# Moving the background decodings of the last two matrices to other units of a three-pass expert kernel

## The chip, the cores and the metric

The kernel runs on one core of a Trainium2 chip. The metric is the time of one execution on the device in microseconds; a version's time is the median over several runs.

## What is computed

Three blocks follow each other: block-causal attention, a mixture of experts whose gate is balanced over the tokens, and a two-matrix block with a SoLU and a layer norm. Only what the change touches is quoted.

```python
def _moe_ref(x, w_gate, w1, w2):          # x 2304 x 512, 8 experts of 512 x 1024 x 512
    ...                                    # P: gate, balanced in 8 rounds
    for e in range(E):
        h = np.maximum(x @ w1[e], 0.0)
        ye = h @ w2[e]
        out += P[:, e:e + 1] * ye

def _moe2_ref(x, w_in, w_out, g_ln):      # w_in 512 x 1024, w_out 1024 x 512
    h = x @ w_in
    ...                                    # SoLU, then layer norm with g_ln
    return (ln @ w_out).astype(np.float32)
```

## The kernel before

**Number format.** TensorE multiplies operands that are split into two parts (a cast and a remainder), three matmuls for each product. `split_weights` makes the two parts: ScalarE casts (L445), GpSimd subtracts (L446).

**The experts.** The tokens go through the experts in three passes of 768 tokens. An expert is halved into two units, so that a pass has the units u = 2 to 15 behind the two that are done with the attention. In every unit the first layer is computed with seven block products in place of eight (`first_layer`, L712): TensorE makes the products (L708 to L710), VectorE combines them (L720, tiles u2, u3, vu2, vu3; the trace cuts the digits), ScalarE copies r1 (L733), and `hidden` makes the hidden tiles. In the first pass these are h tiles (L750 on ScalarE, L751 on VectorE), and the second layer is an ordinary one (`second_layer`, L853: six outputs of twelve matmuls, accumulated by VectorE in L868). In the second and third passes a hidden tile is weighted by the gate into `hb` (L762 on VectorE), combined and split into seven `hf` tiles (L769 on ScalarE, L770 and L773 on GpSimd, one L773 on VectorE), and the second layer has seven products as well (`second_products`, L804): 14 groups of six matmuls, each into a PSUM tile `yps`, which VectorE adds to the accumulator (L816) or, in a pass's first unit, ScalarE copies there (L814).

**Order.** The second products of a unit stand behind the first layer of the next, so that a unit's stretch on TensorE holds 84 matmuls of a first layer and the 84 of the second layer of the unit before. A list of 28 units, `work`, runs through the second and third passes. In between, `finish_pass` combines the accumulators of a pass (L831), multiplies the sums y0 of the first, ordinary units with the gate (L848 on GpSimd) and adds them (L850 on VectorE), and `spread_x` (L599 and others) makes the seven combined token tiles of the next pass. Each engine executes its instructions in the order in which they stand in its queue.

**The decodings.** w_in and w_out of the last block come as 64-bit words. `late` lists 32 half matrices of 128x256 words, 16 of w_in and 16 of w_out. `decode` (L455) makes one of them into the two-part format and stores it to DRAM, from where the last block loads it: a load of 256 KB by SyncE into a tile of the ring `wr` (11 tiles, shared with the weight tiles W, of which a unit takes 14); on VectorE the seven instructions L465, L474, L468, L471, L477, L479, L483 on 128x256, for w_out an eighth, L485; the cast L445 on ScalarE; the subtraction L446 on GpSimd; a store of 256 KB (L488). The scratch tiles a64, b64 and f64 are there once each. Nothing needs a decoded matrix before the last block, from about 1745 us on.

**Who calls it.** The first pass calls it between the layers of a unit (n = u - 2 = 0 to 13), the two later passes behind the first layer of the unit with the number n = 14 to 41:

```python
    def late_decode(n):
        if 8 <= n < 40:
            decode(*late[n - 8])
    ...
        late_decode(u - 2)          # first pass
    ...
            late_decode(n + 14)     # second and third pass
```

So before the change there is one decoding for each n from 8 to 39: n = 8 to 13 in the last six units of the first pass, n = 14 to 27 in the second pass, n = 28 to 39 in all but the last two units of the third.

Of the kernel before, what the change touches and what calls it, by code (L numbers as in the profile page):

```python
# [24 lines left out]
def build(ctx, tc, qT, kT, v, w_gate, w1, w1s, w2, w_in, w_out, g_ln, out):  # L25
# [36 lines left out]
    def r32(ap):  # L62
        return ap.bitcast(F32)
# [380 lines left out]
    def split_weights(t, raw):  # L444
        nc.scalar.copy(t[:, 0, :], raw)  # L445
        nc.gpsimd.tensor_tensor(t[:, 1, :], raw, r32(t[:, 0, :]), op=ALU.subtract)  # L446
# [8 lines left out]
    def decode(i, half, src, scale=None):  # L455


        pair = wr.tile([P, 2, 512], F32R, tag="wr", name="w64")
        raw = pair[:, 0, :].bitcast(U32)
        nc.sync.dma_start(raw, src)  # L460
        raw = raw.rearrange("p (n w) -> p n w", w=2)
        lo, hi = raw[:, :, 0], raw[:, :, 1]
        a = dec.tile([P, 256], U32, tag="a64", name="a64")
        b = dec.tile([P, 256], U32, tag="b64", name="b64")
        nc.vector.tensor_scalar(  # L465
            a, hi, 3, 0x3FFFFFFF, op0=ALU.logical_shift_left, op1=ALU.bitwise_and
        )
        nc.vector.scalar_tensor_tensor(  # L468
            a, hi, 0xC0000000, a, op0=ALU.bitwise_and, op1=ALU.bitwise_or
        )  # L470
        nc.vector.scalar_tensor_tensor(  # L471
            a, lo, 29, a, op0=ALU.logical_shift_right, op1=ALU.bitwise_or
        )
        nc.vector.tensor_scalar(  # L474
            b, lo, 28, 1, op0=ALU.logical_shift_right, op1=ALU.bitwise_and
        )
        nc.vector.tensor_tensor(a, a, b, op=ALU.add)  # L477

        nc.vector.tensor_scalar(  # L479
            b, hi, 1, 28, op0=ALU.logical_shift_left, op1=ALU.logical_shift_right  # L480
        )
        f = dec.tile([P, 256], F32, tag="f64", name="f64")
        nc.vector.scalar_tensor_tensor(f, b, 7.0, r32(a), op0=ALU.is_ge, op1=ALU.mult)  # L483
        if scale is not None:
            nc.vector.tensor_scalar_mul(f, f, scale)  # L485
        t = pair[:, 1, :].rearrange("p (s n) -> p s n", s=2)
        split_weights(t, f)
        nc.sync.dma_start(wdram[i, :, :, half * 256 : half * 256 + 256], r32(t))  # L488
# [473 lines left out]
    late = []  # L962
    for i in range(16):
        for half in range(2):

            if i < 8:
                a = i % 2 * 1024 + half * 512
                late.append((i, half, w_in[i // 2 * P : i // 2 * P + P, a : a + 512]))
            else:
                c = i - 8  # L970
                late.append((i, half, w_out[c * P : c * P + P, half * 512 : half * 512 + 512], gsc[:, c : c + 1]))
    def late_decode(n):
        if 8 <= n < 40:
            decode(*late[n - 8])


    ws = second_weights(2)
    for u in range(2, 16):
        hs = {}
        first_layer(W, X, plain_hidden(hs))  # L980
        if u < 15:
            W, nws = first_factors(u + 1, stg), second_weights(u + 1)
        else:
            X = {}
            run(spread_x(1, X))
            W = load_factors(2, 0)
        late_decode(u - 2)
        second_layer(u, 0, ws, hs)
        ws = nws
# [9 lines left out]
    for n, (p, u) in enumerate([*work, (3, 2)]):  # L999
        if n < len(work):  # L1000
            if u % 2 == 0:
                Pb = gate_weights(u // 2, p)
            R = {}
            hidden, steps = weighted_hidden(R, Pb)
            first_layer(W, X, hidden)
            late_decode(n + 14)

        if before:
            for _ in second_products(*before):
                next(steps, None)  # L1010
        run(steps)
        if n < len(work):
            if n + 1 < len(work):
                if work[n + 1][0] > p:
                    X = {}
                    run(spread_x(p + 1, X))
                W = load_factors(work[n + 1][1], 0)
            before = load_factors(u, 1), R, u == 2
        if u == 2 and p > 1:
            finish_pass(p - 1)  # L1020
# [161 lines left out]
```

## Time and profile before

| | |
|---|---|
| median of three runs | 1983.21 us (1980.9 to 1985.86) |
| the profiled execution | 1983.74 us, its span 1982.0 us |
| TensorE busy | 1898.4 us, 96% of the span |
| VectorE, GpSimd, ScalarE busy | 1454.0, 1163.6, 743.3 us |
| mean granted TensorE clock | 0.985 |

The profile shows one execution. Busy time counts an engine's own instructions; the granted clock is the share of TensorE's full 2.4 GHz that it was given, so that 0.5 is its lower level of 1.2 GHz. The three passes of the units 2 to 15 stand between 472 and 1745 us; the first pass ends at about 905 us, the second at about 1335 us. The trace cuts a digit at the end of a name (hb for hb and y0's slots, w for w64, a and b for a64 and b64).

### The profile page before, as it was taken

How to read it: one execution, taken by the hardware profiler on the slowest of the kernel's cores; microseconds unless marked ns; L12 is line 12 of the kernel's file. 1: busy time of each engine (PE TensorE's matmuls, PEld its weight loads, DVE VectorE, ACT ScalarE, POOL GpSimd, SP SyncE). 2: the span in 40 equal slices, each digit the busy share in tenths (PEclk: the TensorE clock that was granted, in tenths of full speed). 3: DMA queues.
4: the chain of work that ended last, by engine and by line, in shares of the span. 5: the costliest groups of instructions: out<-in, count | busy, mean ns of one | idle time of the engine just before them, and what ended most of it. 6: DMA issues, size and time to landing. Idle time of an engine off the chain costs nothing.

```text
span 1982.0 us, 31143 instructions
## 1 busy us (share of the span) xinstructions
PE 1898.4 (96%) x10487; PEld 1762.7 (89%) x10487; DVE 1454.0 (73%) x3104; ACT 743.3 (38%) x1555; POOL 1163.6 (59%) x920
## 2 busy tenths in 40 slices
PE   5899999889999999999999999998999999989999
PEld 4688998788998989889999999987999999978887
DVE  5868677666777769888867667797866766678774
ACT  5766657433434434343222222222222122224332
POOL 7775645455766667656666676668757557631000
PEclk8999999999999999999999999998999999989999
DMA  8765554337888888879787787876788787851100
GB/s 233 189 181 150 153 148 117 134 99 270 298 303 309 292 315 311 297 251 370 271 289 265 272 279 257 288 259 238 282 285 294 257 278 274 307 205 44 47 28 32
DMA packets 197758, 454.61 MB, mean 229 GB/s; under 512 B 20432, under 2 KB 78432, under 8 KB 197472
## 3 DMA queue, kind: packets, MB, share of 16 engines
q1 hardware_dynamic: 197600, 452.63, 67.3%
q8 instruction: 84, 1.38, 0.3%
q14 instruction: 74, 0.61, 0.1%
HBM read 295.72 MB, written 128.52 MB: 214 GB/s over the span
## 4 chain that ended last, share of the span: by engine, by line
PE 77%; DVE 9%; DMA 4%; POOL 4%; issue 3%; ACT 1%; SPq 1%; DVEq 0%; POOLq 0%; ACTq 0%
PE yps L708 5%; PE yps L710 5%; PE yps L709 5%; PE psb L709 4%; PE psb L708 4%; PE psb L710 4%; PE yps L862 3%; PE yps L864 3%; PE yps L863 3%; PE psc L710 2%; PE psc L708 2%; PE psc L709 2%; PE psa L708 2%; PE psa L710 2%; PE psa L709 2%
## 5 line engine op out<-in xcount | busy, mean ns | idle before, releaser
L770 POOL TENSOR_TENSOR hf<-hb,hf 128x768 fp32r<-128x768 f32 x196 | 368.4, 1895 | 94.9 <-ACT hf L769 94.9
L769 ACT CAST hf<-hb 128x768 fp32r<-128x768 f32 x196 | 160.5, 836 | 490.4 <-POOL hb L773 158.5
L708 PE MATMUL yps<-hf,W 128*128 128x384 f32 x784 | 268.1, 342 | 10.5 <-DVE hb L762 8.2
L709 PE MATMUL yps<-hf,W 128*128 128x384 f32 x784 | 267.1, 341 | 0.0
L710 PE MATMUL yps<-hf,W 128*128 128x384 f32 x784 | 263.8, 341 | 0.0
L773 POOL TENSOR_TENSOR hb<-hb 128x768 f32<-128x768 f32 x84 | 158.8, 1891 | 161.6 <-DVE hb L762 160.1
L816 DVE TENSOR_TENSOR acc<-yps,acc 128x384 f32<-128x384 f32 x364 | 192.6, 549 | 67.6 <-PE yps L710 66.9
L446 POOL TENSOR_TENSOR w<-raw,w 128x512 fp32r<-128x512 f32 x96 | 125.8, 1323 | 109.3 <-ACT w L445 104.6
L708 PE MATMUL psb<-X,W 128*128 128x384 f32 x504 | 169.7, 337 | 1.4 <-ACT acc L814 1.4
L709 PE MATMUL psb<-X,W 128*128 128x384 f32 x504 | 169.3, 336 | 0.0
L710 PE MATMUL psb<-X,W 128*128 128x384 f32 x504 | 167.7, 335 | 0.0
L708 PEld LDWEIGHTS yps<-hf,W 128*128 128x128 f32 x784 | 149.0, 190 | 13.1 <-DVE hb L762 9.8
L709 PEld LDWEIGHTS yps<-hf,W 128*128 128x128 f32 x784 | 149.1, 190 | 0.0
L720 DVE TENSOR_TENSOR u<-psb,r 128x384 f32<-128x384 f32 x168 | 91.1, 550 | 79.1 <-PE psb L710 71.4
L710 PEld LDWEIGHTS yps<-hf,W 128*128 128x128 f32 x784 | 148.7, 190 | 0.0
L862 PE MATMUL yps<-w,h 128*128 128x512 f32 x336 | 133.3, 397 | 5.5 <-DVE acc L868 2.7
L233 POOL TENSOR_SCALAR e<-e,sv 128x128 f32<-128x128 f32 (+2 forms) x144 | 81.1, 567 | 95.6 <-DVE sv L229 31.4
L446 POOL TENSOR_TENSOR W<-raw,W 128x512 fp32r<-128x512 f32 x84 | 117.7, 1416 | 29.7 <-ACT W L445 29.7
L864 PE MATMUL yps<-w,h 128*128 128x512 f32 x336 | 132.6, 395 | 0.0
L863 PE MATMUL yps<-w,h 128*128 128x512 f32 x336 | 132.5, 394 | 0.0
L1102 POOL TENSOR_SCALAR lh<-ln 128x1024 f16<-128x1024 f32 x18 | 19.1, 1059 | 187.4 <-DVE ln L1099 65.2
L708 PE MATMUL psa<-X,W 128*128 128x384 f32 x336 | 113.5, 338 | 2.9 <-ACT W L445 1.5
(233 smaller groups left out, 5330.5 us busy)
## 6 DMA issues: line engine op xcount, KB each, us to landing
W<-fd SPq DMA_DIRECT2D x392, 512.0 KB, 5.6
fd<-W SPq DMA_DIRECT2D x154, 512.0 KB, 5.2
fd<-w SPq DMA_DIRECT2D x84, 256.0 KB, 4.7
raw<-in_w1s SPq DMA_DIRECT2D x56, 256.0 KB, 5.5
raw<-in_w SPq DMA_DIRECT2D x14, 1024.0 KB, 6.9
raw<-in_w SPq DMA_DIRECT2D x40, 256.0 KB, 3.4
kh<-khigh SPq DMA_DIRECT2D x64, 144.0 KB, 2.9
kl<-kraw SPq DMA_DIRECT2D x64, 144.0 KB, 2.7
```

The lines of the kernel that those rows point to most:

```text
L446: nc.gpsimd.tensor_tensor(t[:, 1, :], raw, r32(t[:, 0, :]), op=ALU.subtract)
L708: nc.tensor.matmul(ps, wh, xl, start=start and kc == 0, stop=False, skip_group_check=True)
L709: nc.tensor.matmul(ps, wh, xh, start=False, stop=False, skip_group_check=True)
L710: nc.tensor.matmul(ps, wl, xh, start=False, stop=stop and kc == 1, skip_group_check=True)
L720: nc.vector.tensor_tensor(to, bank[g, a], tmp[g, "r1" if a == "b" else name[1:]], op=ALU.add)
L769: nc.scalar.copy(hi, a)
L770: nc.gpsimd.tensor_tensor(lo, a, r32(hi), op=ALU.subtract)
L773: eng.tensor_tensor(o, a, b, op=ALU.subtract)
L816: nc.vector.tensor_tensor(a, ps, a, op=ALU.add)
L862: nc.tensor.matmul(ps, hl, ws[c][:, 0, :], start=c == 0, stop=False)
L863: nc.tensor.matmul(ps, hh, ws[c][:, 1, :], start=False, stop=False)
L864: nc.tensor.matmul(ps, hh, ws[c][:, 0, :], start=False, stop=c == 3)
```

## The change

Which n has a decoding is now written out in a list. None of the first pass's units (n = 0 to 13) has one, nor have the last unit of the second pass (n = 27) and the first two of the third (n = 28, 29). The last two units (n = 40, 41) have one each, and the seven units n = 16, 18, 20, 22, 24, 33 and 36 two each, whose second stands directly behind the first in the code. The order of the 32 half matrices stays the same. All else of the kernel is unchanged.

```diff
--- before.py
+++ after.py
@@ -969,9 +969,13 @@
                 c = i - 8
                 late.append((i, half, w_out[c * P : c * P + P, half * 512 : half * 512 + 512], gsc[:, c : c + 1]))
+
+    when = sorted([*range(14, 27), *range(30, 42), 16, 18, 20, 22, 24, 33, 36])
+
     def late_decode(n):
-        if 8 <= n < 40:
-            decode(*late[n - 8])
+        for i, w in enumerate(when):
+            if w == n:
+                decode(*late[i])
```

The first place is VectorE's queue in the second unit of the third pass (n = 29), where TensorE makes that unit's first layer and then the second products of n = 28. Before, these rows stood around the last hidden tiles hb of that first layer (psc is one of its PSUM tiles, y0 the sum of the first, ordinary units that finish_pass adds):

```order
L720 TENSOR_TENSOR psc_14656<-psc_14656,u2_14614 128x384
L465 TENSOR_SCALAR a64_14713<-w64_14711 128x256
L474 TENSOR_SCALAR b64_14714<-w64_14711 128x256
L773 TENSOR_TENSOR hb_14368<-hb_14368,hb_14332 128x768
L762 SCALAR_TENSOR_TENSOR hb_14701<-psc_14656,pb_14254 128x384
L468 SCALAR_TENSOR_TENSOR a64_14713<-w64_14711,a64_14713 128x256
L720 TENSOR_TENSOR psc_14667<-psc_14667,u2_14623 128x384
L850 TENSOR_TENSOR acc_101<-acc_101,y0_14579 128x768
L471 SCALAR_TENSOR_TENSOR a64_14713<-w64_14711,a64_14713 128x256
L762 SCALAR_TENSOR_TENSOR hb_14701<-psc_14667,pb_14254 128x384
L477 ISA a64_14713<-a64_14713,b64_14714 128x512
L479 TENSOR_SCALAR b64_14714<-w64_14711 128x256
```

Now the same stretch reads:

```order
L773 TENSOR_TENSOR hb_14336<-hb_14336,hb_14300 128x768
L762 SCALAR_TENSOR_TENSOR hb_14636<-psb_14568,pb_14222 128x384
L720 TENSOR_TENSOR psc_14608<-psc_14608,u2_14566 128x384
L720 TENSOR_TENSOR psc_14619<-psc_14619,u2_14575 128x384
L762 SCALAR_TENSOR_TENSOR hb_14653<-psc_14608,pb_14222 128x384
L762 SCALAR_TENSOR_TENSOR hb_14653<-psc_14619,pb_14222 128x384
L850 TENSOR_TENSOR acc_101<-acc_101,y0_14536 128x768
L720 TENSOR_TENSOR u2_14856<-psb_14849,r1_14838 128x384
```

The decoding's rows are gone. Three of the four L850 now stand further ahead, among the u and vu rows of that unit; the fourth stands behind the last hb.

The second place is VectorE's queue among the second products of a doubled unit. Before, in a unit with one decoding (it stands ahead of these rows), the adds followed each other:

```order
L816 TENSOR_TENSOR acc_101<-yps_10991,acc_101 128x384
L816 TENSOR_TENSOR acc_101<-yps_11002,acc_101 128x384
L762 SCALAR_TENSOR_TENSOR hb_10958<-psc_10924,pb_10541 128x384
L816 TENSOR_TENSOR acc_101<-yps_11010,acc_101 128x384
L816 TENSOR_TENSOR acc2_10038<-yps_11021,acc2_10038 128x384
L816 TENSOR_TENSOR acc2_10038<-yps_11029,acc2_10038 128x384
```

Now, in the unit n = 18, the second decoding's rows stand between the adds:

```order
L816 TENSOR_TENSOR acc_101<-yps_11236,acc_101 128x384
L465 TENSOR_SCALAR a64_11215<-w64_11213 128x256
L474 TENSOR_SCALAR b64_11216<-w64_11213 128x256
L816 TENSOR_TENSOR acc_101<-yps_11247,acc_101 128x384
L762 SCALAR_TENSOR_TENSOR hb_11188<-psc_11154,pb_11074 128x384
L816 TENSOR_TENSOR acc_101<-yps_11255,acc_101 128x384
L468 SCALAR_TENSOR_TENSOR a64_11215<-w64_11213,a64_11215 128x256
L816 TENSOR_TENSOR acc2_9948<-yps_11266,acc2_9948 128x384
L471 SCALAR_TENSOR_TENSOR a64_11215<-w64_11213,a64_11215 128x256
L816 TENSOR_TENSOR acc2_9948<-yps_11274,acc2_9948 128x384
L477 ISA a64_11215<-a64_11215,b64_11216 128x512
L816 TENSOR_TENSOR acc2_9948<-yps_11287,acc2_9948 128x384
```

From the second add on there is a decoding row after nearly every add, until the seven are through; the first decoding stands where the single one stood. The seven doubled units read alike, but for L485 behind the seven in n = 33 and 36 (w_out), and n = 16, whose first decoding stands a row or two further behind.

The third place is ScalarE's queue at the beginning of the second pass, around the cast L445 of the decoding n = 15; L814 are the copies of that pass's first accumulators. Before:

```order
L814 COPY acc2_10038<-yps_10454 128x384
L814 COPY acc2_10038<-yps_10462 128x384
L445 CAST w64_10360<-f64_10370 128x256
L814 COPY acc_101<-yps_10474 128x384
L814 COPY acc_101<-yps_10482 128x384
L814 COPY acc_101<-yps_10493 128x384
L814 COPY acc_101<-yps_10501 128x384
L733 COPY r1_10550<-psa_10543 128x384
```

Now:

```order
L814 COPY acc2_9948<-yps_10344 128x384
L445 CAST w64_10270<-f64_10280 128x256
L814 COPY acc2_9948<-yps_10352 128x384
L769 CAST hf_10361<-hb_10243 128x768
L814 COPY acc2_9948<-yps_10364 128x384
L814 COPY acc2_9948<-yps_10372 128x384
L814 COPY acc_101<-yps_10384 128x384
L814 COPY acc_101<-yps_10392 128x384
L814 COPY acc_101<-yps_10403 128x384
L814 COPY acc_101<-yps_10411 128x384
L733 COPY r1_10460<-psa_10453 128x384
L733 COPY r1_10469<-psa_10462 128x384
```

The cast stands three copies further ahead: seven of the fourteen L814 are behind it, before the change four, and both r1 copies of the next unit stand behind it in either order.

## Rows read from the trace of the kernel before

**Rows 1.** The page: busy time and share by engine; one costly group

```profile
PE 1898.4 (96%) x10487; PEld 1762.7 (89%) x10487; DVE 1454.0 (73%) x3104; ACT 743.3 (38%) x1555; POOL 1163.6 (59%) x920
...
L770 POOL TENSOR_TENSOR hf<-hb,hf 128x768 fp32r<-128x768 f32 x196 | 368.4, 1895 | 94.9 <-ACT hf L769 94.9
```

**Rows 2.** Single units: window, length, busy time by engine, granted clock, DMA

```profile
943.20:975.10 31.90, 30.14 (x170) 29.17 (x168) 26.44 (x35) 8.24 (x14) 23.36 (x13) 1.00 0.78 278
...
1034.40:1063.80 29.40, 29.40 (x170) 29.40 (x170) 20.38 (x40) 6.56 (x10) 18.31 (x12) 1.00 0.72 236
...
1269.20:1303.00 33.80, 31.54 (x171) 30.80 (x170) 29.73 (x45) 12.43 (x21) 25.91 (x16) 0.95 0.73 234
1303.00:1334.80 31.80, 30.24 (x170) 29.26 (x169) 28.68 (x53) 6.47 (x12) 17.37 (x12) 1.00 0.78 278
1334.80:1378.40 43.60, 34.51 (x169) 32.82 (x168) 37.53 (x36) 11.09 (x21) 40.25 (x21) 0.88 0.64 232
```

**Rows 3.** TensorE's waits from 905 to 1745 us: total, times, longest

```profile
PE yps L708 <- DVE hb L762: 8.2, 4, 4.3
PE yps L708 <- DVE acc L816: 2.3, 1, 2.3
PE psb L708 <- ACT acc L814: 1.4, 1, 1.4
```

**Rows 4.** VectorE groups, 1034.4 to 1063.8: count, busy, mean ns, idle before

```profile
L816 DVE TENSOR_TENSOR acc<-yps,acc 128x384 f32<-128x384 f32 x14 | 7.5, 553 | 3.2 <-PE yps L710 3.2
...
L477 DVE CUSTOM_DVE_ANT_0 a<-a,b 128x512 uint16<-128x512 uint16 x1 | 0.4, 410 | 0.0
```

**Rows 5.** Timeline of TensorE: matmuls that begin after a wait, its length in brackets

```profile
794.73 0.50 PE L862 MATMUL yps<-w,h 128*128 128x512 f32 x1 [0.84 <-DVE acc L868]
...
852.34 0.50 PE L862 MATMUL yps<-w,h 128*128 128x512 f32 x1 [2.45 <-DVE h L751]
...
1351.98 0.45 PE L708 MATMUL psc<-X,W 128*128 128x384 f32 x1 [1.07 <-DVE vu L720]
...
1357.52 0.44 PE L708 MATMUL yps<-hf,W 128*128 128x384 f32 x1 [2.27 <-DVE hb L762]
...
1362.89 0.44 PE L708 MATMUL yps<-hf,W 128*128 128x384 f32 x1 [1.49 <-DVE hb L762]
...
1369.53 0.69 PE L708 MATMUL yps<-hf,W 128*128 128x384 f32 x1 [4.25 <-DVE hb L762]
```

**Rows 6.** Stretches behind three of these waits: columns as in rows 2

```profile
852.50:856.00 3.50, 3.50 (x10) 2.96 (x11) 3.50 (x5) 2.45 (x5) 3.50 (x4) 0.54 1.04 423
1358.00:1361.50 3.50, 3.40 (x11) 2.89 (x9) 3.50 (x4) 0.00 (x0) 3.35 (x2) 0.52 0.94 337
1368.00:1375.00 7.00, 5.47 (x17) 5.48 (x18) 6.31 (x7) 0.58 (x2) 4.74 (x4) 0.51 0.34 102
```

**Rows 7.** Timeline of VectorE at the end of the first pass: start, length, line

```profile
849.38 1.04 DVE L471 SCALAR_TENSOR_TENSOR a<-w,a 128x256 uint32<-128x256 uint32 x1
```

**Rows 8.** Timeline of VectorE between second and third pass

```profile
1358.32 1.35 DVE L465 TENSOR_SCALAR a<-w 128x256 uint32<-128x256 uint32 x1
1359.59 1.90 DVE L474 TENSOR_SCALAR b<-w 128x256 uint32<-128x256 uint32 x1
...
1362.76 1.81 DVE L468 SCALAR_TENSOR_TENSOR a<-w,a 128x256 uint32<-128x256 uint32 x1
...
1364.96 2.10 DVE L850 TENSOR_TENSOR acc<-acc,y 128x768 f32<-128x768 f32 x1
1366.98 2.02 DVE L471 SCALAR_TENSOR_TENSOR a<-w,a 128x256 uint32<-128x256 uint32 x1
```

**Rows 9.** Timeline of VectorE, decoding n = 16 among the adds of its unit

```profile
964.80 1.99 DVE L465 TENSOR_SCALAR a<-w 128x256 uint32<-128x256 uint32 x1
...
973.01 1.61 DVE L477 CUSTOM_DVE_ANT_0 a<-a,b 128x512 uint16<-128x512 uint16 x1
...
975.68 0.41 DVE L483 SCALAR_TENSOR_TENSOR f<-b,a 128x256 f32<-128x256 uint32 x1
```

**Rows 10.** Timeline of VectorE at the end of a steady unit

```profile
1096.51 0.56 DVE L720 TENSOR_TENSOR u<-psb,r 128x384 f32<-128x384 f32 x1 [2.63 <-PE psb L710]
```

## The prediction

> **What bounds the kernel now.** I read the page first: TensorE is busy 96% of the span [rows 1], so the change can only win back time in which TensorE stands or runs at its lower clock. Next I cut the two later passes into units and compared their lengths. An undisturbed unit takes 29.4 us, all of it TensorE at full clock, with VectorE busy 20.4 of it; the units that are longer are the first of the second pass (31.9), and the last of the second pass with the two behind it: 33.8, 31.8 and 43.6 [rows 2]. So (33.8 - 29.4) + (31.8 - 29.4) + (43.6 - 29.4) = 21.0 us are lost around the change from the second to the third pass, and 2.5 at the beginning of the second.
>
> Then I asked the waits who is late. From 905 to 1745 us TensorE's largest wait by far is for hidden tiles hb of VectorE (8.2 us in 4 waits), then for an add of VectorE (2.3) and for a copy of ScalarE (1.4) [rows 3]; none of the eight kinds in that view is for a transfer. The timeline gives the places: 1.07 and 2.27 us ahead of 1357.5, then 1.49 and 4.25 up to 1369.5 [rows 5]. Behind the longer of these stops (2.27 and 4.25 us, and 2.45 in the first pass) stands a stretch of some 3.5 to 5.5 us of matmuls in which the granted clock is 0.52, 0.51 and 0.54, the lower of its two levels [rows 6], while the short stops (0.84, 1.07, 1.49) have no such row. A stop of over two microseconds is thus paid twice: matmuls of 3.4 busy us cost about 1.6 more than at full clock, those of 5.5 about 2.7.
>
> Last, VectorE in those places. An instruction of a decoding takes 0.41 us where GpSimd is idle [rows 4] and up to 2.0 where it is not [rows 8, 9]: GpSimd's own instruction there takes 1.9 [rows 1]. Between the passes the decoding's L465, L474, L468 and L471 took 1.35 + 1.90 + 1.81 + 2.02 = 7.1 us [rows 8], and the hidden tiles stood behind them in VectorE's queue.
>
> **First pass: six decodings removed.** The stop of 0.84 us (a VectorE add is late) and the one of 2.45 (a VectorE h tile) [rows 5] stand behind decodings: in the second one L471 alone took 1.04 us, the instructions around it much the same [rows 7]. Without them I give the first back whole, with its restart 1.0 us; the second gives 2.6 and, from 3.5 us at 0.54 of the clock [rows 6], 3.5 x 0.46 = 1.6 more: 4.2. **Gain 5.2**; at least 3, if the ordinary work of that place (L658, L664, L720) still makes VectorE a microsecond late, and at most these 5.2.
>
> **n = 27 removed.** Its unit loses 4.4 us, of which 2.3 are the stop for an add [rows 2, 3] and the rest the restart at the lower clock; the next one loses 2.4, in which the decoding's backlog and spread_x share. I take the first whole and two thirds of the second: **gain 6.0**; bounds 3 (spread_x alone keeps VectorE late) and 6.8.
>
> **n = 28 and 29 removed.** The unit of 43.6 us loses 14.2: stops of 1.07 + 2.27 + 1.49 + 4.25 = 9.1 us, 1.6 + 2.7 at the lower clock, and some 0.8 in four restarts. The first two stops (up to 1357.5) end before n = 29's first instruction at 1358.3 [rows 5, 8]; they come from finish_pass, which the change only reorders, so I keep them with the lower clock behind the second: 1.07 + 2.27 + 1.6 + 0.4 = 5.4. The other two I give back whole, since 7.1 us of decoding stand there against 5.7 us of waiting: **gain 14.2 - 5.4 = 8.8**. The L850 of 2.10 us stays in that queue [rows 8]; if it and a reordered L850 behind GpSimd's L848 are late instead, the gain is 4; if the whole stall goes, 14.2.
>
> **Beginning of the second pass.** The wait of 1.4 us for a copy of ScalarE [rows 3] is a copy queued behind the cast L445, which waits for VectorE's decoding n = 15. In the new order seven copies are queued behind that cast, before four. VectorE reaches the decoding about one L773 earlier, which offsets part. **Loss 1.0**; bounds 0 and 3 (three copies' groups of six matmuls are 3.1 us).
>
> **Seven doubled units.** The second decoding stands among the adds, where GpSimd is busy without a pause. The nearest row is n = 16 of before, whose single decoding stood in the same place: the first, the fifth and the last of its seven instructions took 1.99, 1.61 and 0.41 us, and all of it lasted from 964.8 to 976.1 [rows 9], 11.3 us, of which six adds and an hb at 0.55 [rows 4] took 3.9, so that the decoding has about 7.5. Its unit lost 31.9 - 29.4 = 2.5 us, 1.4 of it in the wait already counted; the rest, 1.1, is the most that I charge to the decoding. A single decoding in its usual place costs nothing (29.4) [rows 2]; its cover is VectorE's idle time, 3.2 us among fourteen adds of 0.55 [rows 4] and 2.63 ahead of the next u [rows 10]. 7.5 us exceed the 3.2 + 2.6 of cover by 1.7, which is less than two groups of six matmuls (1.05 us each), and VectorE may be late by that much while TensorE still has free PSUM tiles. I take 0.5 us a unit, between the single unit and the 1.1, for the last adds have no decoding row between them: **loss 3.5**; bounds 0 and 7.7.
>
> The Trainium skill's page "SBUF — State Buffer" (Who interferes with whom) says that VectorE with two operands in SBUF, or in a two-port mode, and GpSimd exclude each other, the second to issue blocked for the whole of the other's instruction. That speaks against the doubled units: by it each of the seven would wait out a GpSimd instruction, and the sum is that of rival (c) below. The trace agrees where L465 takes 1.99 us, but not for the last one's 0.41.
>
> **The rest.** Two more slots of `wr` and two transfers of 256 KB fall into the doubled units; no transfer ends a wait of TensorE in the stretch [rows 3], so 0. If they came late, a weight tile of the fourteen in 29.4 us is one slot, 2.1 us, nearer to its use. n = 40 and 41 get what the unit of 29.4 us had at no loss: 0, at most 1.1 each. n = 14's decoding moves to the end of the first pass, where n = 12 and 13 had theirs: 0.
>
> **Sum** against the profiled execution, 1983.74 us: -5.2 - 6.0 - 8.8 + 1.0 + 3.5 = -15.5, which gives **1968 us**. The median of before, 1983.21, is 0.5 lower, well inside the runs' spread. Differences under 0.3% (6 us) can hardly be told from no change here.
>
> **The rivals.**
> (a) *The transition stays late.* VectorE executes in order and four L850 of 2.1 us each wait for GpSimd's L848; three of them now stand ahead of u and vu rows. For it: the stops ahead of 1357.5 are theirs. Against: VectorE has at least the 7.1 us of decoding less. Gains 4.2 + 4.4 + 4, losses 1 + 5: 1977.
> (b) *All stalls go.* With the decodings gone VectorE comes early to the transition, so that the first two stops vanish as well, and the doubled units cost nothing: -5.2 - 6.8 - 14.2 = 1957.5. For it: VectorE's 29.7 and 28.7 busy us in the two units ahead [rows 2]. Against: finish_pass's own L850 and L848.
> (c) *Doubled units stall TensorE.* If all seven instructions take GpSimd's 1.9 us, VectorE has 13 us of decoding and 7.7 of adds in fourteen groups of 1.05, 14.7 us: 6.0 late, less 2.63 of idle time [rows 10], a stop of 3.4, and behind it 1.6 at the lower clock. 5.0 x 7 = 35 against gains of 20.0 - 1.0: 1999.7. It decides from a backlog at which a stop passes two microseconds. Against: n = 16 had 7.5 us, not 13, and GpSimd itself waits for the second f in its queue, which ends the contention.
> (d) *The work removed is not what TensorE waits for*, since L599, L831 and L850 keep VectorE just as late: gains of 4 in the first pass alone, losses of 4: about 1984.
>
> **How the numbers follow.** Forecast 0.55 (1962 to 1975), (a) 0.2, (b) 0.14, (c) 0.06, (d) 0.05. The range leaves out (c), (d) and half of (b): **1958 to 1979**. Faster: the forecast, (b) and three quarters of (a), 0.84; same: the rest of (a) and (d), 0.10; slower: (c), 0.06. By the page's rule alone (c) would hold; the row of 0.41 us is why it has little.
>
> **What would show it.** First pass: no wait for h of L751 and no lower clock near 850 us. Transition: the units of 33.8, 31.8 and 43.6 us become about 29.4, 30.2 and 35. Beginning of the second pass: a wait for L814 of 2 to 3 us in place of 1.4. Doubled units of 29.4 to 30.5 us, VectorE's last adds late. The prediction is wrong if a doubled unit takes over 32 us, or if the hidden tiles between the passes are still waited for by over 5 us.

## The result

The changed kernel takes 1997.41 us (median of 5 runs, 1993.92 to 2004.84), the kernel before 1983.21 (5 runs, 1980.9 to 1985.88): a ratio of 1.0075, 95% interval 1.0057 to 1.0093. It is slower by some 14 us where 15.5 us of gain were forecast; 1997.4 lies above the range of 1958 to 1979.

The page of the changed kernel, span and busy time [rows 1]:

```profile
span 1992.7 us, 31164 instructions
...
PE 1904.7 (96%) x10487; PEld 1766.3 (89%) x10487; DVE 1467.0 (74%) x3104; ACT 742.2 (37%) x1555; POOL 1166.9 (59%) x920
```

TensorE's busy time is 6.3 us longer for the same 10487 matmuls. The mean granted clock is 0.985 in either profile, so a lower clock does not explain the difference of the whole. TensorE's waits from 905 to 1760 us [rows 3]; each row is total, times, longest:

```profile
PE psa L708 <- DVE acc L816: 8.2, 8, 1.6
PE psa L708 <- ACT acc L814: 3.1, 1, 3.1
PE yps L708 <- DMA W<-fd: 2.5, 1, 2.5
PE yps L708 <- issue: 2.5, 1, 2.5
PE psa L708 <- DVE hb L762: 2.0, 1, 2.0
PE psb L708 <- DVE u L720: 1.9, 1, 1.9
```

The wait for hb, 8.2 us before, is down to one of 2.0 and three small ones (1.3 in all). In its place stand eight waits of the next unit's first products psa for an add, a long one for a copy, one for a weight tile, and one for which the profile has no releaser.

Single units, columns as in [rows 2]; the last line is a stretch within one of them:

```profile
940.90:975.60 34.70, 31.55 (x170) 30.79 (x169) 25.90 (x40) 10.52 (x19) 23.86 (x14) 0.95 0.74 261
975.60:1008.60 33.00, 31.37 (x170) 30.85 (x169) 25.62 (x50) 8.14 (x13) 20.83 (x14) 0.95 0.75 254
...
1038.50:1071.10 32.60, 31.29 (x168) 30.97 (x169) 24.11 (x48) 8.80 (x13) 21.94 (x14) 0.95 0.72 250
...
1160.70:1191.80 31.10, 29.77 (x169) 29.45 (x170) 24.27 (x48) 8.69 (x13) 22.01 (x14) 1.00 0.76 262
1281.60:1311.00 29.40, 29.40 (x171) 29.40 (x170) 26.57 (x39) 11.25 (x20) 21.30 (x13) 1.00 0.77 275
1311.00:1345.10 34.10, 31.47 (x170) 30.86 (x170) 27.15 (x43) 7.96 (x13) 22.13 (x14) 0.95 0.68 238
1345.10:1379.40 34.30, 31.60 (x170) 30.80 (x169) 28.36 (x28) 10.15 (x19) 32.53 (x16) 0.95 0.78 280
...
1499.00:1531.80 32.80, 30.08 (x168) 29.34 (x169) 23.69 (x50) 7.23 (x11) 17.80 (x11) 1.00 0.79 297
1041.30:1044.70 3.40, 3.40 (x12) 3.40 (x12) 2.07 (x5) 2.04 (x4) 3.40 (x3) 0.54 0.78 271
```

The units of the change of passes, 33.8, 31.8 and 43.6 us before, now take 29.4, 34.1 and 34.3. n = 16, near the beginning of the second pass, takes 34.7 us (before 31.9), and the unit behind a doubled one 33.0 (n = 17), 32.6 (n = 19) or 31.1 (n = 23) in place of 29.4: the second decoding stands among the adds, and the first products of the next unit pay for it. The doubled unit n = 18 itself takes 29.9.

To see where the time went, I compared the start of the matmul with the same number in both traces (both have 10487). Number 4032 lies some four units ahead of the end of the first pass and 4620 at its end, 4900 in n = 16 of the second, behind the cast of n = 15, 6500 behind that pass's doubled units, 7400 behind the change of passes, 9200 ahead of the last block:

```
matmul number     2400    4032    4620    4900    6500    7400    9200   10486
before           445.5   775.0   901.5   952.6  1233.0  1412.6  1727.5  1977.8
after            446.0   773.9   893.5   953.0  1245.4  1413.1  1734.7  1988.6
gained or lost    +0.5    -1.6    -6.8    +8.4   +11.9   -11.8    +6.7    +3.5
forecast                          -5.2    +1.0    +2.5   -14.8    +1.0     0
```

Up to 4032 the kernel before has one decoding (n = 8, at 754 us) and the changed kernel none. Of the -1.6 there I make nothing: three kernels below that keep n = 8 (h1, h2, h3) gained 1.5 there as well. So the -1.1 up to 4032 is taken as scatter. The gains came, 6.8 and 11.8 us. But 8.4 were lost at the beginning of the second pass, 18.6 in the doubled units, and 3.5 in the last block. The sum is +10.7 for the two profiled executions (spans 1992.7 and 1982.0); the medians are 14.2 apart.

**A doubled unit.** VectorE's timeline in n = 18, the second decoding alone (the adds between are left out, but for the last line):

```profile
1028.65 0.77 DVE L465 TENSOR_SCALAR a<-w 128x256 uint32<-128x256 uint32 x1
1029.34 1.94 DVE L474 TENSOR_SCALAR b<-w 128x256 uint32<-128x256 uint32 x1
...
1032.60 1.36 DVE L468 SCALAR_TENSOR_TENSOR a<-w,a 128x256 uint32<-128x256 uint32 x1
...
1034.35 1.60 DVE L471 SCALAR_TENSOR_TENSOR a<-w,a 128x256 uint32<-128x256 uint32 x1
...
1036.34 1.60 DVE L477 CUSTOM_DVE_ANT_0 a<-a,b 128x512 uint16<-128x512 uint16 x1
...
1038.34 1.45 DVE L479 TENSOR_SCALAR b<-w 128x256 uint32<-128x256 uint32 x1
...
1040.17 0.41 DVE L483 SCALAR_TENSOR_TENSOR f<-b,a 128x256 f32<-128x256 uint32 x1
1040.51 2.87 DVE L816 TENSOR_TENSOR acc<-yps,acc 128x384 f32<-128x384 f32 x6
```

The seven took 9.1 us; the seven of the unit's first decoding, ahead of the adds, took 2.5. The difference goes with GpSimd, which had stood idle for 8.11 us during the first decoding and then worked without a pause until 1039.6:

```profile
1027.42 1.85 POOL L773 TENSOR_TENSOR hb<-hb 128x768 f32<-128x768 f32 x1 [8.11 <-DVE hb L762]
```

The whole traces of the two kernels say the same: of their 448 decoding instructions (without L485) 106 took over 0.6 us, and each of these lay beside a GpSimd instruction for at least 63% of its time; of the 342 shorter ones 323 lay beside none. No run took GpSimd's work away, so this rests on the traces alone.

At 1040.51 six adds followed each other. TensorE, which had begun the next unit, waited for two adds, that of 1037.87 and then the first of the six (the third line is the same place two doubled units on, behind n = 22):

```profile
1038.47 0.44 PE L708 MATMUL psa<-X,W 128*128 128x384 f32 x1 [0.34 <-DVE acc L816]
...
1041.10 0.45 PE L708 MATMUL psa<-X,W 128*128 128x384 f32 x1 [1.31 <-DVE acc L816]
...
1163.35 0.45 PE L708 MATMUL psa<-X,W 128*128 128x384 f32 x1 [1.33 <-DVE acc L816]
```

That stop of 1.3 us was paid again: behind it stands a stretch with a granted clock of 0.54 (the line 1041.30 above), the lower level, which costs some 1.6 us.

**The beginning of the second pass.** TensorE's waits, and then the instructions of VectorE and ScalarE that came late:

```profile
909.51 0.44 PE L708 MATMUL psa<-X,W 128*128 128x384 f32 x1 [1.98 <-DVE hb L762]
...
945.30 0.44 PE L708 MATMUL psa<-X,W 128*128 128x384 f32 x1 [3.15 <-ACT acc L814]
```

```profile
908.90 1.02 DVE L762 SCALAR_TENSOR_TENSOR hb<-psa,pb 128x384 f32<-128x384 f32 x2 [3.88 <-DMA pb<-pd]
```

```profile
943.35 0.41 ACT L445 CAST w<-f 128x256 fp32r<-128x256 f32 x1 [6.33 <-DVE f L483]
```

TensorE came to the second pass 8 us earlier (matmul 4620), but the gate's load pb landed only 0.9 us earlier (908.87 for 909.73): VectorE sat idle for 3.88 us until then, and TensorE waited 1.98. Why pb was not earlier is to be read from SyncE's queue. There it stands behind loads of spread_x (L607), which waited 5.6 us for the L599 that VectorE makes among the rows of the decoding n = 14, and right behind that decoding's store:

```profile
900.46 0.53 SPq L488 DMA_DIRECT2D wd<-w  x1
901.08 1.22 SPq L822 DMA_DIRECT2D pb<-pd  x2
```

Then the cast of n = 15 held ScalarE for 6.33 us until VectorE had its f. It came 3.8 us earlier than before (943.35 for 947.13), less than half of TensorE's 8; seven copies stood behind it in place of four, and TensorE waited 3.15 where it had waited 1.45.

**A load late in VectorE's queue.** Behind the doubled unit n = 33 VectorE waited 6.04 us for the load of the next decoding, with combinations of the first layer queued behind it; in the same microseconds TensorE stood for 2.46:

```profile
1518.49 0.29 DVE L465 TENSOR_SCALAR a<-w 128x256 uint32<-128x256 uint32 x1 [6.04 <-DMA w<-in_w_out]
```

```profile
1520.68 0.41 PE L708 MATMUL yps<-hf,W 128*128 128x384 f32 x1 [2.46 <-issue]
```

**The last block.** VectorE's timeline around its first h, and TensorE's:

```profile
1757.24 2.54 DVE L850 TENSOR_TENSOR acc<-acc,y 128x768 f32<-128x768 f32 x1 [1.24 <-POOL acc L831]
1759.71 0.54 DVE L816 TENSOR_TENSOR acc<-yps,acc 128x384 f32<-128x384 f32 x1
```

```profile
1760.35 0.77 PE L1069 MATMUL h<-w,x 128*128 128x512 f32 x1 [4.07 <-issue]
```

The L850 of the last finish_pass now stands ahead of the last add in VectorE's queue, waited for GpSimd and took 2.54 us. The first h begins just behind that add, after a wait of 4.07 us that the kernel before does not have.

### The profile page after: what moved, and what is told of

It is laid out like the page before. It is cut to its first block, busy times and chain, and to the rows that moved or that the text cites. A ratio compares the mean times of both kernels' runs of the same rounds, so it can differ in the third digit from the quotient of the medians.

```text
span 1992.7 us, 31164 instructions
## 1 busy us (share of the span) xinstructions
PE 1904.7 (96%) x10487; PEld 1766.3 (89%) x10487; DVE 1467.0 (74%) x3104; ACT 742.2 (37%) x1555; POOL 1166.9 (59%) x920
## 4 chain that ended last, share of the span: by engine, by line
PE 75%; DVE 11%; DMA 7%; POOL 2%; issue 2%; ACT 1%; SPq 1%; POOLq 0%; ACTq 0%; DVEq 0%
PE yps L708 4%; PE yps L709 4%; PE yps L710 4%; PE psb L708 4%; PE psb L709 4%; PE psb L710 4%; PE yps L862 4%; PE yps L863 4%; PE yps L864 4%; PE psa L708 3%; PE psa L710 2%; PE psa L709 2%; PE psc L708 2%; PE psc L710 2%; PE psc L709 2%
## 5 line engine op out<-in xcount | busy, mean ns | idle before, releaser
L816 DVE TENSOR_TENSOR acc<-yps,acc 128x384 f32<-128x384 f32 x364 | 191.5, 548 | 52.7 <-PE yps L710 52.1
L708 PE MATMUL psb<-X,W 128*128 128x384 f32 x504 | 171.6, 340 | 2.5 <-DVE u L720 2.2
L709 PE MATMUL psb<-X,W 128*128 128x384 f32 x504 | 171.0, 339 | 0.0
L710 PE MATMUL psb<-X,W 128*128 128x384 f32 x504 | 169.5, 339 | 0.0
L708 PEld LDWEIGHTS yps<-hf,W 128*128 128x128 f32 x784 | 147.3, 188 | 10.4 <-issue 5.7
L709 PEld LDWEIGHTS yps<-hf,W 128*128 128x128 f32 x784 | 147.4, 188 | 0.0
L710 PEld LDWEIGHTS yps<-hf,W 128*128 128x128 f32 x784 | 147.2, 188 | 0.0
```

What stands on the lines that cost most here:

```text
L708: nc.tensor.matmul(ps, wh, xl, start=start and kc == 0, stop=False, skip_group_check=True)
L709: nc.tensor.matmul(ps, wh, xh, start=False, stop=False, skip_group_check=True)
L710: nc.tensor.matmul(ps, wl, xh, start=False, stop=stop and kc == 1, skip_group_check=True)
L816: nc.vector.tensor_tensor(a, ps, a, op=ALU.add)
```

## The experiments

My theory after the result: the doubled units cost 18.6 us since the second decoding meets a busy GpSimd among the adds; the gain of the emptied first pass is given back at the beginning of the second pass; the change of passes did gain. The rivals were that the loss lies in the places left empty or in the last units, not in the doubling. The runs e1 to e4, h1 to h3 and k1 set the list `when` alone, of which the new line is shown; of the other edits the main lines are shown. In f1, f2 and f4 `decode` takes a further place `also`, to which it stores its result a second time. The medians of before were 1983.5 to 1985.1 in the several sessions; ratios are to it.

**Only the change of passes emptied (e1).**

```diff
-    when = sorted([*range(14, 27), *range(30, 42), 16, 18, 20, 22, 24, 33, 36])
+    when = sorted([*range(7, 27), *range(30, 42)])
```

> One decoding for each n = 7 to 26 and 30 to 41: the kernel before, with its three decodings at n = 27 to 29 moved to n = 7, 40 and 41; no unit has two. Theory (the seven doubled units make VectorE's adds late and cost about 18.6 us, the emptied change of passes gives 11.8 us): 1983.2 - 11.8 = 1971 us. Rival A (the last two units' decodings cost the 3.5 us by which the last block began later in the changed kernel): 1975 us. Rival B (the change of passes gained only because VectorE came to it from time lost earlier): within 4 us of 1983.

1979.32 us, ratio 0.9971 (0.9959 to 0.9982). Faster, but by 5.8 and not 12: by matmul numbers the change of passes gained 9.1 and the last block lost 2.9. The median alone lies within rival B's 4 us of 1983; against before of the same session it does not, and the 9.1 us were gained with no time lost ahead of them (matmul 6500 came 1.1 us earlier than before), so rival B falls.

**The first pass's decodings earlier (e2).**

```diff
+    when = sorted([*range(0, 6), *range(14, 40)])
```

> The six decodings of the first pass moved from n = 8 to 13 to n = 0 to 5, all others as before. The trace of the changed kernel gained 6.9 us up to the end of the first pass and lost 8.4 at the beginning of the second. Theory (both belong to the end of the first pass without decodings, whatever comes later): 1983.2 - 6.9 + 8.4 = 1985 us, and n = 0 to 5 cost nothing. Rival C (the 8.4 us come from the doubled unit n = 16): 1976 us.

1998.58 us, ratio 1.0061 (1.0049 to 1.0073). Neither theory: up to matmul 4032 it lost 9.9 us where the changed kernel gained 1.6, about 1.9 for each of the six, in stops, most of them ahead of 780 us, where the kernel before has none from 500 us on (the rows go up to 900 us):

```profile
PE yps L862 <- DVE h L751: 3.7, 4, 2.1
PE yps L862 <- DVE acc L868: 3.5, 4, 1.3
```

These units were not free places, which I had taken for granted. Behind them it gained 4.9 and lost 5.8, as the theory says, without any doubled unit; so rival C falls.

**Only the last two units (e3).**

```diff
+    when = sorted([*range(8, 38), 40, 41])
```

> The decodings of n = 38 and 39 moved to n = 40 and 41, all others as before. Rival A (decodings in the last two units delay the last block's loads): 1986.7 us, and TensorE's wait ahead of its first h in the last block is about 4 us longer. Theory (that difference is the scatter of the last block's loads): 1983 us within 2.

1986.71 us, ratio 1.0009 (1.0 to 1.0018): between 0 and 3.6 us slower, both expectations within reach. Its trace has the wait of 4.1 us ahead of the first h, as rival A says, and 4.0 us lost behind matmul 9200, though the change of passes, which this list leaves as it was, lost 2.2 as well.

**The seven second decodings in the first pass (e4).**

```diff
+    when = sorted([*range(0, 7), *range(14, 27), *range(30, 42)])
```

> The changed kernel without a doubled unit: its seven second decodings stand in the first pass at n = 0 to 6. Theory (the seven cost 18.6 us and nothing else changes): 1997.4 - 18.6 = 1979 us, or up to 3 more where n = 0 to 6 meet a busy GpSimd. Rival (the loss lies in the beginning of the second pass and in the last block, which stay): 1997 us less at most 4.

1996.4 us, ratio 1.0051 (1.0038 to 1.0064). The total agrees with the rival. The trace does not: the doubled units' 18.6 us fell to 3.2 - 0.4 = 2.8, and n = 0 to 6 cost 12.9 in their place. So the next runs take the work away instead of moving it.

**The second decodings left out (f1).**

```diff
+            if w == n and (i == 0 or when[i - 1] != n):
+                twice = when[i + 1 : i + 2] == [n]
+                decode(*late[i], also=late[i + 1][:2] if twice else None)
```

> The changed kernel, where the seven second decodings are not computed: the result of the unit's first one is stored in both places, so that only the load and the work on VectorE, ScalarE and GpSimd fall away. Theory (VectorE's late adds in the seven units cost 11.9 us in the second pass and 6.7 in the third): 1997.4 - 18.6 = 1979 us, every one of these units at 29.4 us. Rival (the stores and the ring's slots cost it, a load late in VectorE's queue): at least 1990 us.

1978.38 us, ratio 0.9977 (0.9968 to 0.9986), 19.0 us below the changed kernel, as the theory said. The units n = 18 and 19 together, and n = 33 and 34, columns as in [rows 2]:

```profile
1008.40:1067.20 58.80, 58.80 (x338) 58.67 (x337) 38.54 (x80) 13.76 (x21) 37.91 (x23) 1.00 0.82 284
1462.30:1521.10 58.80, 58.80 (x338) 58.80 (x338) 41.22 (x82) 14.48 (x21) 39.52 (x24) 1.00 0.81 283
```

They take 58.8 us, twice 29.4, with the same stores; by matmul numbers the two stretches of the doubled units lost nothing (-0.5 and -0.4 in place of 11.9 and 6.7). The cost is the second decoding's load, its slot of the ring and its work, not its store. What of it is the load and the slot was not separated, but the stops behind the adds are VectorE's work by the timeline above, and only that of 2.46 us behind n = 33 goes with a load.

**The first pass's decodings left out (f2).**

```diff
-        if 8 <= n < 40:
-            decode(*late[n - 8])
+        if 14 <= n < 40:
+            decode(*late[n - 8], also=late[n - 17][:2] if 17 <= n < 23 else None)
```

> The kernel before, where the six decodings n = 8 to 13 are not computed; the results of n = 17 to 22 are stored in two places instead. Theory (an emptied first pass comes earlier to the second pass by 6.9 us and meets a gate load and ScalarE's cast that come no earlier, so that most is given back): 1983.2 - 6.9 + 5 = 1981 us, with a wait for hb behind the load of pb near 905 us. Rival (the gain stays whole): 1976 us.

1985.06 us, ratio 1.0007 (0.9998 to 1.0017): not even the expected 2 us were left. It gained 6.8 us up to matmul 4620 and lost 8.4 up to 4900, the very numbers of the changed kernel. TensorE's waits from 840 to 960 us (lines are 3 further on):

```profile
PE psa L711 <- ACT acc L817: 3.1, 1, 3.1
PE psa L711 <- DVE hb L765: 2.0, 1, 2.0
```

These are the waits for the copy behind the cast and for hb behind the gate's load. As the second pass begins now, the six decodings of the first pass cost the kernel before nothing, although TensorE waited 2.45 us behind one of them [rows 5].

**Both decodings ahead of the adds (f3).**

```diff
-        a = dec.tile([P, 256], U32, tag="a64", name="a64")
-        b = dec.tile([P, 256], U32, tag="b64", name="b64")
+        a = pair[:, 1, 0:256].bitcast(U32)
+        b = pair[:, 1, 256:512].bitcast(U32)
...
-    dec = ectx.enter_context(tc.tile_pool(name="dec", bufs=1, side="left"))
+    dec = ectx.enter_context(tc.tile_pool(name="dec", bufs=2, side="left"))
```

> The changed kernel with the scratch tiles a64 and b64 in the unused half of the ring tile, and f64 twice, so that a unit's two decodings no longer wait for each other's scratch and stand in VectorE's queue interleaved, ahead of most adds. Theory (the place among the adds, where GpSimd is busy, makes the second decoding long): the second decodings take under 5 us instead of about 9, the doubled units come down to 29.4 to 30.5 us, and the time to 1997.4 - 12 = 1985 us or below. Rival (two decodings are too much for a unit wherever they stand): 1995 us or more.

1999.39 us, ratio 1.0084 (1.0071 to 1.0097): the rival's number, in four runs. The two decodings did become shorter, 8.1 us together in n = 20 (n = 18 had 11.6), but now they stood ahead of the adds. VectorE's timeline in n = 20, and TensorE's wait:

```profile
1085.76 1.96 DVE L477 CUSTOM_DVE_ANT_0 w<-w 128x512 uint16<-128x512 uint16 x1
...
1089.58 0.54 DVE L816 TENSOR_TENSOR acc<-yps,acc 128x384 f32<-128x384 f32 x1
...
1092.58 0.55 DVE L816 TENSOR_TENSOR acc<-yps,acc 128x384 f32<-128x384 f32 x1
```

```profile
1090.17 0.44 PE L708 MATMUL yps<-hf,W 128*128 128x384 f32 x1 [1.35 <-DVE acc L816]
```

TensorE stops in the middle of the second products in place of their end. The doubled unit is too full in either order, by 1.6 us in n = 20 and 22 (n = 18, at 29.7 us, lost only 0.3). The stretch of the second pass's doubled units lost 8.7 us in place of 11.9, so the order gives a part back; it was taken again by the stop behind n = 33, now 4.87 us, and by 5.1 us less gained at the change of passes.

**n = 14 and 15 left out (f4).**

```diff
+            if w == n and n >= 16:
+                decode(*late[i], also={4: late[0][:2], 7: late[1][:2]}.get(i))
```

> The changed kernel, where n = 14 and 15 are not computed; the results of n = 17 and 19 are stored in two places instead. Theory (of the 8.4 us that the changed kernel loses at the beginning of the second pass, about 1.5 are spread_x behind n = 14 and about 4.9 ScalarE's cast of n = 15, the rest the gate load): 1997.4 - 6 = 1991 us, the wait for hb behind pb's load stays at 2 us or grows. Rival (the beginning is late whatever is decoded there): 1997 us within 2.

1995.35 us, ratio 1.0062 (1.0044 to 1.008), 2 us below the changed kernel and within the runs' spread: by the time the rival. By matmul numbers the beginning lost nothing (-0.2 in place of +8.4), as the theory says. Its other half failed: the wait for hb behind pb's load, which was to stay, is gone. Without the decoding n = 14 pb was issued at 900.01 us, 4.3 behind matmul 4620 in place of 7.6, and landed 3.3 us earlier by that measure. But the doubled units lost 15.1 + 11.8 in place of 11.9 + 6.7, so only 2 us of the gain were kept. Why they lost more, the two stores behind n = 17 and 19 or the earlier arrival, was not tried.

**Which of n = 27, 28 and 29 (h1, then h2).**

```diff
+    when = [*range(8, 27), 28, *range(30, 42)]
```

> The kernel before, with only the decodings of n = 27 and 29 moved, to n = 40 and 41; the first pass and n = 28 as before, no unit with two. Theory (n = 27 and 29 are what the change of passes loses to the decodings, n = 28, whose instructions took under 0.45 us, costs nothing): as much gained at the change as with all three away, 9 to 12 us, and no first pass n = 7 (1.9 us): 1973 to 1977 us. Rival (n = 28 blocks the change as well): 1980 us or more.

1978.02 us, ratio 0.9973 (0.9963 to 0.9984); 8.5 us gained at the change of passes, 2.5 lost in the last block, so that the time lies 1 us above the theory's range. The gain is about that with all three away (9.1): n = 28 cost nothing that stands out of the scatter.

```diff
+    when = [*range(8, 27), *range(29, 42)]
```

> The kernel before, with the decodings of n = 27 and 28 moved to n = 40 and 41, n = 29 as before. Theory (n = 29 alone holds the hidden tiles of the 43.6 us unit, n = 27 costs 4 to 6): 1979 us within 2, and the hidden tiles are still waited for by over 4 us. Rival (n = 27's backlog made the stall of n = 29): 1973 to 1976 us.

1985.26 us, ratio 1.0008 (0.9998 to 1.0019); the change of passes gained nothing (+0.5), and both expectations missed. Without n = 27 TensorE no longer stops for its adds and runs into a weight tile's load instead:

```profile
1307.44 0.66 PE L708 MATMUL yps<-hf,W 128*128 128x384 f32 x1 [3.68 <-DMA W<-fd]
```

So the 4.4 us that I had read off n = 27's unit are not n = 27's to give. In the unit n = 29 the waits for hb fell to 0.80 and 1.80 us, and matmul 7190 came 6.3 us earlier than before; but just behind it TensorE stood for 5.02 us. The profile has no releaser for that; in ScalarE's queue the cast L445 of n = 29 had waited 7.09 us for VectorE's f up to 1373.9, with four copies L814 behind it, and TensorE went on at 1374.8. So with n = 29 in place its decoding holds the change of passes by one path or another; whether n = 27 adds anything to n = 29's gain was not separated.

**One doubled unit alone (h3).**

```diff
+    when = sorted([*range(8, 27), *range(30, 42), 20])
```

> The kernel of one decoding for each n = 7 to 26 and 30 to 41, with n = 7's moved to n = 20, the only unit with two. Theory (a doubled unit costs 1.2 to 2.9 us also when it is alone, the early first-pass one 1.9): within 1.5 us of that kernel's 1979.3, and the unit n = 20 takes 1.2 us or more over 29.4. Rival (the doubled units cost only since several follow each other): 2 us below, and n = 20 takes 29.4 us.

1981.18 us, ratio 0.9986 (0.9975 to 0.9997), 1.9 above the kernel with n = 7 in its place (3 by the ratios of the two sessions), so beyond the 1.5 that I had allowed. The unit n = 20, and the one behind it:

```profile
1064.80:1094.70 29.90, 29.51 (x170) 29.18 (x168) 23.95 (x40) 6.29 (x9) 19.32 (x12) 1.00 0.84 302
1094.70:1125.70 31.00, 29.68 (x168) 29.36 (x169) 24.03 (x48) 8.43 (x13) 20.47 (x13) 1.00 0.71 248
```

The doubling costs 0.5 us in its own unit, where I had expected 1.2 or more, and 31.0 - 29.4 = 1.6 in the next, also when it is alone; the unit behind that is back at 29.4. The rival falls.

**The last block's order restored (k1).**

```diff
+    when = [*range(7, 27), 28, *range(30, 41)]
```

> The kernel before, with the decoding of n = 27 moved to n = 7 and that of n = 29 to n = 40; n = 41 has none, no unit has two. In every kernel with decodings at both n = 40 and 41 one L850 of the last finish_pass stands ahead of the last add in VectorE's queue; here it stands behind it, as in the kernel before. Theory (that L850 makes the last block's first h wait 4.1 us for a PSUM tile, net some 2.5 to 4): no such wait, and 1978.0 - 3 + 1.9 (n = 7) = 1977 us within 2. Rival (a decoding in the last units delays the last block whatever the order): the wait of 4.1 us stays, 1979 us or more.

1977.47 us, ratio 0.9965 (0.9952 to 0.9979), the lowest median, though not clear of e1 and h1. TensorE's wait for the first h of the last block:

```profile
PE h L1069 <- issue: 0.3, 1, 0.3
```

The 4.1 us are 0.3, with 1.4 for an add just ahead, and the stretch behind matmul 9200 lost 0.9. The ten kernels with decodings at n = 40 and 41 all have one L850 ahead of the last add, and lost 2.5 to 4.1 there (mean 3.4); before and the three others have it behind, and these three lost 0.9, 1.0 and 2.5 (e2). So about 2 us are to be put to that order, less than the wait itself. A decoding at n = 40 alone leaves the order as it was; with both, the planner, which orders the instructions of each queue, drew L850 ahead of the add. Against h1 the change of passes gained only 5.4 of 8.5 in this trace, with a stop of 2.73 us for a copy of ScalarE in the unit n = 30 (1.36 in h1); why was not tried.

## Why the prediction was wrong

**The doubled units: the step that failed first.** "I take 0.5 us a unit", 3.5 in all, with 7.7 as the upper bound; they cost 18.6, 2.7 a unit. The mechanism was named and rival (c) priced it at 35. The term was mis-sized in three steps.

First, the row that I weighed it by was read too low. I gave the decoding n = 16 of before [rows 9] "about 7.5" us, by taking six adds and an hb off its 11.3. These are the four of its seven instructions that the rows leave out:

```profile
966.71 1.93 DVE L474 TENSOR_SCALAR b<-w 128x256 uint32<-128x256 uint32 x1
...
969.49 1.14 DVE L468 SCALAR_TENSOR_TENSOR a<-w,a 128x256 uint32<-128x256 uint32 x1
...
971.02 1.60 DVE L471 SCALAR_TENSOR_TENSOR a<-w,a 128x256 uint32<-128x256 uint32 x1
...
975.01 0.28 DVE L479 TENSOR_SCALAR b<-w 128x256 uint32<-128x256 uint32 x1
```

With 1.99, 1.61 and 0.41 they are 9.0 us, as long as the 9.1 of n = 18; between them stand five adds and an hb. By my own sum 9.0 exceeds the cover of 5.8 by 3.2, which is 1.1 more than two groups of six matmuls; as an estimate from these rows that would have been a stop of about 1.1 us in each doubled unit. The stops that came behind those of the second pass are 0.9 to 1.65 us.

Second, n = 16 stood alone in its unit. It began 10.3 us ahead of the next unit and ended 1.0 behind that unit's beginning, with no stop. The second decoding of n = 18 began 9.8 us ahead and ended 2.1 behind. "1.1 is the most that I charge" was thus read from one unit that ended inside the cover. Behind n = 16 and 18 stops of 1.6 and 1.3 us came with a lower granted clock (0.95 over the unit).

Third, "the row of 0.41 us" was my reason against rival (c), and it is none. GpSimd stood idle for 2.27 us when that instruction ran, from 975.68 to 976.09:

```profile
976.61 0.74 POOL L446 TENSOR_TENSOR w<-f,w 128x256 fp32r<-128x256 f32 x1 [2.27 <-ACT w L445]
```

The runs f1 and h3 show the cost, f3 that the order within the unit gives back only a part. My sign for it was ill placed: n = 18 took 29.9 us, inside the 29.4 to 30.5 that I had forecast for a doubled unit, and the loss stood in the unit behind it (32.6). Only n = 16, at 34.7 us with the stop for the copy in it, passed the 32 that I had named.

**The first pass: right in its stretch, nothing in the sum.** "Gain 5.2": 6.8 came, though a wait of 1.53 us for an h of L751 stands in it, at 878 us. But 8.4 were given back at once, because what TensorE meets there, the gate's load and the cast of n = 15, came only 0.9 and 3.8 us earlier where TensorE came 8. f2 shows this without a doubled unit and with the change of passes as it was; its only other edit is six further stores in n = 17 to 22. I had priced the beginning of the second pass as a shift of three copies (1.0, at most 3) and n = 14's move at 0, and did not ask what an earlier TensorE would meet. f4 shows that the 8.4 us go with n = 14 and 15, the wait for the gate's load included; but its doubled units lost 8.3 us more, so that the whole gained only 2.

**n = 27: wrong.** "Gain 6.0": h2 gives 0 for n = 27 and 28 together with n = 29 in place, and in the changed kernel the two units of 33.8 and 31.8 us became 29.4 and 34.1, a gain of 2.1. The lost time of that unit was real, but the load of a weight tile was next in line (2.49 us in the changed kernel, 3.68 in h2).

**n = 28 and 29: right.** "Gain 8.8": h1 gained 8.5 with n = 27 and 29 away. The unit of 43.6 became 34.3, as forecast (35); the stop that stayed was one of 1.9 us for u, behind a reordered L850.

**The last block: missed.** I priced it at 0. In the changed kernel's queue one L850 stands ahead of the last add, and I did not ask who waits for that add. The stretch lost 3.5 us, of which about 2 are that order's (k1 and the comparison there).

**The page's rule.** By the exclusion of VectorE and GpSimd in the Trainium skill's page "SBUF — State Buffer" (Who interferes with whom), each of the seven that meets a GpSimd instruction would wait it out. The trace agrees: six of the seven in n = 18 took 0.77 to 1.94 us, each beside GpSimd instructions for some nine tenths of its time or all of it, and the last took 0.41 us while GpSimd was idle. Rival (c) was too dear at 13 us for the seven all the same, for they took 9.1.

The sum by measured terms: -1.1 - 6.8 + 8.4 + 18.6 - 11.8 + 3.5 = 10.8, the spans' 10.7.

## What to carry to other kernels

Background work has a price by place: before moving it, read from the unit what cover is left after what already stands there, not from another unit that had more. A stop that is removed ahead of a hand-over (a gate load, a first copy, a weight tile) is worth only what the next-latest at that hand-over allows, so ask of each gain who comes next, and whether that one also comes earlier. When a planner rewrites the queues, look at each changed row far from the edit too: one L850 ahead of one add took back about 2 us of the 8.5 that the good part of this change gives.

## What was unexpected in the hardware

Behind n = 18 a stop of 1.31 us, with another of 0.34 shortly before it, was followed by 3.4 us at the lower clock (0.54); a stop of 1.33 us behind n = 22 was not, the clock of its whole unit being 1.00. Nor was the stop of 2.46 us behind n = 33 (clock 1.00 from 1520.6 to 1524.0). So my "over two microseconds" holds in neither direction, and these rows do not say what decides.

Not every instruction of VectorE was long beside GpSimd: the adds L816 between the decoding's rows, which read one operand from PSUM, took 0.54 us beside a busy GpSimd in n = 18, as they do elsewhere (0.55 [rows 4]).

Two traces of different kernels can agree to about 0.1 us over hundreds of microseconds where their programs agree (the kernel with only n = 38 and 39 moved stays within 0.1 of its +0.4 up to matmul 6500), so that stretches can be compared more finely than medians. They need not: h1 and h2 have the same first pass and differ by 2.3 us in its end, and through the last block and the change of passes such pairs differ by one or two. Differences of that size between two stretches show nothing by themselves.
